# One Trainium2 kernel re-planned: engine order from an in-kernel list scheduler, DMA transposes, and attention outputs computed in column tiles

## Chip, cores, metric

One core of one Trainium2 chip. The metric is device time in microseconds (us) of one launch. Medians are quoted with the range of the runs. The record calls a run slow when it lies over 1.5% above the fastest run of its kernel in the same call.

Engine names in the profile: PE is TensorE's matmul stream, PEld its weight loads, DVE is VectorE, ACT is ScalarE, POOL is GpSimd, SP is SyncE.

## The reference, cut to what matters

Two branches read the same x (2048 tokens of 512) and are mixed by a gate per token. All inputs are bf16.

```python
def reference(A_x, A_wq, A_wk, A_wv, A_wo, A_beta, B_x, B_W_gate, B_W_up, B_W_down, gate_w):
    # branch A: 32 heads of 16, four segments of 512 tokens
    for s in range(4):
        logits = einsum('bhqd,bhkd->bhqk', qs, ks) * scale + mask    # causal, within the segment
        a_dot  = einsum('bhqk,bhkd->bhqd', softmax(logits), vs)
        pq     = phi(qs)                                 # phi(t) = t+1 if t>0 else exp(t)
        a_mem  = (pq @ M) / (pq @ z + 1e-6)              # recall from the state so far
        o      = g * a_mem + (1.0 - g) * a_dot           # g = sigmoid(beta), per head
        M, z   = M + phi(ks)^T @ vs, z + sum(phi(ks))    # the state
    a = concat(o) @ wo
    # branch B: a gated feed-forward of width 1792
    b = (relu(x @ W_gate) * (x @ W_up)) @ W_down
    g = sigmoid((x * gate_w).sum(-1, keepdims=True))     # per token
    return g * a + (1 - g) * b
```

Three groups of work follow from this. Dense matmuls are the projections, the feed-forward and the output projection. Attention is the scores ("QK"), their exponential, and the product with V ("PV"). The rest is the state, its recall, and the norm. A "unit" is one segment and one group of eight heads; there are 16.

## The kernel before: the parts that the change touches

PV uses the exponentials as weights and streams V (17 columns, one of them ones, which gives the softmax denominator). The norm and a matmul that transposes its result follow for each of 64 blocks.

```python
        for qb in range(4):
            ndt = psum.tile([P, NDT], F32, name="ndt", tag="X", bufs=2)
            # ... recall matmul into ndt, for segments after the first
            for hl8 in range(8):
                for kb in range(qb + 1):
                    nc.tensor.matmul(ndm[:, 0, hl8, 0:DH + 1],
                                     lhsT=E[kb][:, es, (qb - kb) * P:(qb - kb + 1) * P],
                                     rhs=st["Vp"][:, kb, h, 0:DH + 1], start=first, stop=last)
            # ... VectorE: + eps, reciprocal, * gate, * numerator, sum  ->  o_sb
            nc.tensor.matmul(trp, lhsT=o_sb.rearrange("p h e -> p (h e)"),
                             rhs=diag16[:, t, :], start=True, stop=True)
            nc.vector.tensor_copy(oT[:, c, qb * P:(qb + 1) * P], trp)
```

phi(K) for the state needs tokens on partitions, so K is projected a second time, with x as the weight:

```python
            for t in range(4):
                for ci in range(NC):
                    nc.tensor.matmul(ps[:], lhsT=xT[:, ci, s0 + t * P:s0 + (t + 1) * P],
                                     rhs=wk_sb[:, ci, :], start=(ci == 0), stop=(ci == NC - 1))
                # ... exponential, min, max-add  ->  pK
```

x is transposed by 64 matmuls, and the loads are spread over three queues:

```python
    load_x(nc.sync, 0)
    load_w_piece(nc.scalar, wq_sb, A_wq, 0, D)
    load_w_piece(nc.scalar, wk_sb, A_wk, 0, D)
    load_w_piece(nc.scalar, wv_sb, A_wv, 0, D)
    load_w_piece(nc.sync, wg_sb, B_W_gate, *FP[0])
    load_w_piece(nc.sync, wu_sb, B_W_up, *FP[0])
    load_x(nc.gpsimd, 1)
    # ... the other pieces alternate between the SP and the GpSimd queue
```

The order of each engine's instructions is chosen by the framework, from the order in which the program writes them.

The softmax here doesn't subtract the row's maximum and nothing guards it: scores larger than these inputs give would overflow.

## Time and profile before

| | before |
|---|---|
| time, median (range) | 354.35 us (354.02 to 354.99) |
| span of the profiled run, mean granted clock | 351.7 us, 0.993 |
| busy: PE / DVE / ACT / POOL | 308.4 / 229.1 / 198.0 / 90.5 us |
| first dense matmul at full supply | after a 5.0 us wait that ends at 19.03 us |

How to read it: the span is from the first instruction to the last of the core; the reported time is a little longer (1.7 to 2.0 us in the runs for which both are on record). TensorE is the fullest engine. Its busy time counts a dense matmul of 512 columns as 0.38 us in this trace, while the next one starts after 0.216 us, so a full TensorE must be read from the distance between starts. The lines are in the prediction below.

### The profile page before, as it was taken

How to read it: one execution, taken by the hardware profiler on the slowest of the kernel's cores; microseconds unless marked ns; L12 is line 12 of the kernel's file. 1: busy time of each engine (PE TensorE's matmuls, PEld its weight loads, DVE VectorE, ACT ScalarE, POOL GpSimd, SP SyncE). 2: the span in 40 equal slices, each digit the busy share in tenths (PEclk: the TensorE clock that was granted, in tenths of full speed). 3: DMA queues.
4: the chain of work that ended last, by engine and by line, in shares of the span. 5: the costliest groups of instructions: out<-in, count | busy, mean ns of one | idle time of the engine just before them, and what ended most of it. 6: DMA issues, size and time to landing. Idle time of an engine off the chain costs nothing.

```text
span 351.7 us, 7235 instructions
## 1 busy us (share of the span) xinstructions
PE 308.4 (88%) x2941; PEld 148.1 (42%) x2992; DVE 229.1 (65%) x684; ACT 198.0 (56%) x187; POOL 90.5 (26%) x153
## 2 busy tenths in 40 slices
PE   3489988899999799898999988888999989989984
PEld 2133343335444344334644444334544444444452
DVE  2557959788422756989835575899845386766253
ACT  1306578755843687831754577841764378886300
POOL 6000343341321424310231144230231133242300
PEclk9989999999999999999999999999999999999999
DMA  7991100001000000001000000000000000000000
GB/s 195 357 335 55 61 2 0 2 1 62 3 16 16 32 2 0 2 0 61 2 2 17 30 18 3 0 2 0 2 3 17 30 17 2 0 2 3 0 32 30
DMA packets 10209, 12.39 MB, mean 35 GB/s; under 512 B 593, under 2 KB 9313, under 8 KB 10177
## 3 DMA queue, kind: packets, MB, share of 16 engines
q1 hardware_dynamic: 7584, 6.82, 6.1%
q0 software_dynamic: 1008, 3.55, 3.3%
q10 hardware_dynamic: 1584, 1.57, 1.4%
q8 instruction: 23, 0.38, 0.4%
q14 instruction: 10, 0.07, 0.1%
HBM read 9.84 MB, written 2.10 MB: 34 GB/s over the span
## 4 chain that ended last, share of the span: by engine, by line
PE 52%; DVE 30%; ACT 7%; DMA 5%; issue 3%; POOL 0%; SPq 0%; DVEq 0%; ACTq 0%
PE acc L398 14%; PE ups L383 9%; PE gps L378 7%; PE ndt L317 6%; DMA wu_sb<-in_B_W_up_dram 5%; PE sp L255 4%; DVE hT L388 4%; DVE tb L339 3%; DVE osb L411 3%; PE ps_proj L242 2%; PE ndt L343 2%; PE acc L408 2%; DVE coef L337 2%; PE ps_proj L230 2%; DVE rsb L335 2%
## 5 line engine op out<-in xcount | busy, mean ns | idle before, releaser
L383 PE MATMUL ups<-xT,wu_sb 128*128 128x512 bf16 x210 | 62.7, 382 | 7.1 <-DMA wu_sb<-in_B_W_up_dram 5.0
L378 PE MATMUL gps<-xT,wg_sb 128*128 128x512 bf16 x205 | 59.8, 380 | 2.3 <-DMA wg_sb<-in_B_W_gate_dram 1.0
L388 DVE TENSOR_TENSOR hT<-ups,rg 128x512 bf16<-128x512 f32 x56 | 38.3, 684 | 24.2 <-PE ups L383 18.5
L387 ACT ACTIVATE rg<-gps 128x512 bf16<-128x512 f32 x56 | 33.5, 598 | 35.7 <-PE gps L378 27.8
L398 PE MATMUL acc<-wd_sb,hT 128*128 128x512 bf16 x217 | 50.3, 379 | 0.9 <-DVE osb L411 0.2
L398 PEld LDWEIGHTS <-hT 128*128 128x128 bf16 x224 | 21.5, 98 | 25.3 <-issue 1.2
L383 PEld LDWEIGHTS <-wu_sb 128*128 128x128 bf16 x224 | 20.1, 98 | 25.5 <-DMA wu_sb<-in_B_W_up_dram 5.5
L345 DVE CAST oT<-ndt 128x128 bf16<-128x128 f32 x64 | 18.3, 286 | 16.4 <-PE ndt L343 16.4
L411 DVE TENSOR_SCALAR osb<-acc,ngcol 128x512 bf16<-128x512 f32 x16 | 12.0, 750 | 22.5 <-PE acc L408 22.5
L378 PEld LDWEIGHTS <-wg_sb 128*128 128x128 bf16 x224 | 18.3, 97 | 18.2 <-issue 3.7
L343 PE MATMUL ndt<-diag_134,o_sb 128*128 128x128 bf16 x64 | 14.5, 226 | 11.4 <-DVE o_sb L342 9.8
L333 DVE TENSOR_TENSOR dsb<-ndt,epsvec 128x16 f32<-128x16 f32 x48 | 8.1, 169 | 24.2 <-PE ndt L317 23.7
L255 PE MATMUL sp<-QTsb,KTe 32*128 32x512 bf16 (+3 forms) x256 | 21.7, 304 | 0.7 <-issue 0.2
L339 DVE TENSOR_TENSOR tb<-ndt,coef 128x256 bf16<-128x256 f32 x48 | 20.2, 421 | 1.3
L255 PE MATMUL sp<-QTsb,KTo 32*128 32x512 bf16 (+3 forms) x256 | 20.2, 299 | 0.6 <-ACT E_3100 L276 0.2
L408 PE MATMUL acc<-wo_sb,oT 128*128 128x512 bf16 x60 | 17.8, 380 | 2.3 <-DVE oT L345 1.9
L218 PE MATMUL ps_proj<-xT,wk_sb 128*128 128x512 bf16 x64 | 17.1, 396 | 2.3 <-DVE KTe L221 0.9
L242 PE MATMUL ps_proj<-wv_sb,xT 128*128 128x512 bf16 x62 | 15.7, 379 | 2.6 <-DVE pK L236 1.1
L343 PEld LDWEIGHTS <-o_sb 128*128 128x128 bf16 x64 | 6.1, 95 | 27.6 <-DVE o_sb L342 23.1
L204 PE MATMUL ps_proj<-xT,wq_sb 128*128 128x512 bf16 x61 | 17.1, 393 | 0.5
L255 PEld LDWEIGHTS <-KTe 32*128 32x128 bf16 x256 | 7.1, 91 | 24.1 <-issue 22.9
L207 DVE CAST QTsb<-ps_proj 128x512 bf16<-128x512 f32 x16 | 10.8, 685 | 3.8 <-PE ps_proj L204 3.8
(468 smaller groups left out, 708.6 us busy)
## 6 DMA issues: line engine op xcount, KB each, us to landing
out_dram<-osb SPq DMA_DIRECT2D x16, 128.0 KB, 1.7
xn<-in_A_x_dram POOLq DMA_DIRECT2D x3, 512.0 KB, 3.8
wd_sb<-in_B_W_down_dram POOLq DMA_DIRECT2D x2, 640.0 KB, 12.4
wg_sb<-in_B_W_gate_dram SPq DMA_DIRECT2D x2, 512.0 KB, 14.2
wu_sb<-in_B_W_up_dram SPq DMA_DIRECT2D x2, 512.0 KB, 18.2
wg_sb<-in_B_W_gate_dram SPq DMA_DIRECT2D x2, 384.0 KB, 13.2
wu_sb<-in_B_W_up_dram SPq DMA_DIRECT2D x2, 384.0 KB, 8.8
xn<-in_A_x_dram SPq DMA_DIRECT2D x1, 512.0 KB, 4.9
```

What stands on the lines that cost most here:

```text
L242: nc.tensor.matmul(ps[:], lhsT=xT[:, ci, s0 + t * P:s0 + (t + 1) * P], rhs=wv_sb[:, ci, :], start=(ci == 0), stop=(ci == NC - 1))
L255: nc.tensor.matmul(out_ap, lhsT=ktile[32 * j:32 * j + 32, c, kb * P:(kb + 1) * P], rhs=st["QTsb"][32 * j:32 * j + 32, c, kb * P:kb * P + N ...
L317: nc.tensor.matmul(ndm[:, 0, hl8, 0:DH + 1], lhsT=E[kb][:, es, (qb - kb) * P:(qb - kb + 1) * P], rhs=st["Vp"][:, kb, h, 0:DH + 1], start=f ...
L339: nc.vector.tensor_tensor(tb[:], ndm[:, :, :, 0:DH], coef[:, :, :, None].to_broadcast([P, 2, 8, DH]), ALU.mult)
L343: nc.tensor.matmul(trp, lhsT=o_sb.rearrange("p h e -> p (h e)"), rhs=diag16[:, t, :], start=True, stop=True)
L378: nc.tensor.matmul(gps[:], lhsT=wg_sb[:, ci, fv * P:(fv + 1) * P], rhs=xT[:, ci, s0:s0 + L], start=(ci == 0), stop=(ci == NC - 1))
L383: nc.tensor.matmul(ups[:], lhsT=wu_sb[:, ci, fv * P:(fv + 1) * P], rhs=xT[:, ci, s0:s0 + L], start=(ci == 0), stop=(ci == NC - 1))
L387: nc.scalar.activation(rg[:], gps[:], ACT.Relu)
L388: nc.vector.tensor_tensor(hT[:, fv, :], ups[:], rg[:], ALU.mult)
L398: nc.tensor.matmul(acc[:], lhsT=hT[:, fv, lc:lc + P], rhs=wd_sb[:, fv, :], start=(fv == 0), stop=False)
L408: nc.tensor.matmul(acc[:], lhsT=oT[:, ci, lc:lc + P], rhs=wo_sb[:, ci, :], start=False, stop=(ci == NC - 1))
L411: nc.vector.tensor_scalar(osb[:], acc[:], ngcol[:, tt:tt + 1], None, ALU.mult)
```

## The change

Its intent: take work off TensorE's stream (second K projection, most transposes of x, the transposes of the normalised output), get PV done four heads at a time, move the norm off TensorE's path, and replace the framework's ordering by a plan. The kernel describes each piece of work as an operation with assumed durations, dependences and buffers. A list scheduler inside the kernel plans all engines, and the instructions are then emitted in that order with the framework's own ordering switched off ("pinned").

The diff replaces nearly the whole file. Its core, with cuts marked:

```diff
+class Sched:                       # list scheduler: engines, dependences, buffers, mode changes
+    LAT = {"PE": 0.30, "ACT": 0.12, "DVE": 0.12, "POOL": 0.15, "SP": 0.0, "ACTQ": 0.0}
+    # ... run(): earliest start first; TensorE by key, a change of tile mode costs SW = 0.1
...
+    def c_dummy(e):                # TensorE: ten matmuls on zeros while the loads come
+        for _ in range(10):
+            nc.tensor.matmul(g_dummy.t[:], lhsT=zero[:, 0:P], rhs=zero[:], start=True, stop=True)
...
+    lw["wq"] = loadw("wq", wq_sb, A_wq, 0, D, -200, eng="ACT")      # order: x0, wq, wk, wv, then
+    lw["wk"] = loadw("wk", wk_sb, A_wk, 0, D, 1)                    # gate/up pieces, x1, wo, wd
...
+            nc.sync.dma_start_transpose(out=xT[s].t[:], in_=x[s * L:(s + 1) * L, :])   # s = 1..3
...
-                    nc.tensor.matmul(ps[:], lhsT=xT[:, ci, s0 + t * P:s0 + (t + 1) * P],
-                                     rhs=wk_sb[:, ci, :],             # second K projection
+                nc.sync.dma_start_transpose(out=pK[s].t[:, :, c * P:(c + 1) * P], in_=src.t[:])
...
-                    nc.tensor.matmul(ndm[:, 0, hl8, 0:DH + 1],
-                        lhsT=E[kb][:, es, (qb - kb) * P:(qb - kb + 1) * P],
-                        rhs=st["Vp"][:, kb, h, 0:DH + 1], start=first, stop=last)
+                for kb, src, off, w in ((0, ea, 0, 512), (1, ebf, 0, 384),
+                                        (2, ec, 256 * r, 256), (3, ebf, 384, 128)):
+                    for j in range(4):
+                        h = 8 * c + 2 * j + r
+                        nc.tensor.matmul(g.t[32 * j:32 * j + 32, L - w:L],
+                                         lhsT=Vp[s].t[:, kb, h * HP:h * HP + 32],
+                                         rhs=src.t[:, j, off:off + w],
+                                         start=(kb == 0), stop=(kb == 3), tile_position=(0, 32 * j))
...
-            nc.tensor.matmul(trp, lhsT=o_sb.rearrange("p h e -> p (h e)"),
-                             rhs=diag16[:, t, :], start=True, stop=True)
+                    nc.vector.transpose(T.t[:, r, :, :].rearrange("p b e -> p (b e)"), g.t[:])
+            # ... reciprocal, * gate, * numerator on VectorE, then
+            nc.vector.transpose(dst.t[:], Oa.t[:].rearrange("p b r e -> p (b r e)"))
...
+    order = sc.run()
+    with tc.manual_schedule():
+        for o in order:
+            o.emit(o.eng)
```

In the changed kernel's profile, L439 are projections and gate/up matmuls, L574 the down projection, L584 the output projection, L625 the scores, L656 PV, L670 the recall, L518 the state, L343 the transposes of x by TensorE, L261 the matmuls on zeros; L635 is the exponential, L561 the product of gate and up, L689 VectorE's transpose from PSUM.

## The prediction

> **What bounds the kernel now.** I read the page's busy line first, then the busy slices, then the table of stretches, the matmul timeline and the list of waits.
>
> ```profile
> PE 308.4 (88%) x2941; PEld 148.1 (42%) x2992; DVE 229.1 (65%) x684; ACT 198.0 (56%) x187; POOL 90.5 (26%) x153
> PE   3489988899999799898999988888999989989984
> PEclk9989999999999999999999999999999999999999
> ```
>
> TensorE is busy in nearly every slice, and its granted clock is full. But a modelled matmul time (380 ns for 512 columns) overlaps the next one, so 308 us is not work. The timeline gives the true pace:
>
> ```profile
> 120.77 0.23 PE L343 MATMUL ndt<-diag_134,o_sb 128*128 128x128 bf16 x1 [1.40 <-DVE o_sb L342]
> 120.84 1.03 PE L378 MATMUL gps<-xT,wg_sb 128*128 128x512 bf16 x4
> 121.70 0.81 PE L383 MATMUL ups<-xT,wu_sb 128*128 128x512 bf16 x3
> ...
> 128.68 0.81 PE L378 MATMUL gps<-xT,wg_sb 128*128 128x512 bf16 x2
> 129.42 0.29 PE L255 MATMUL sp<-QTsb,KTe 32*128 32x256 bf16 x4
> 129.54 0.28 PE L255 MATMUL sp<-QTsb,KTo 32*128 32x256 bf16 x4
> 129.75 0.39 PE L378 MATMUL gps<-xT,wg_sb 128*128 128x512 bf16 x1
> ```
>
> Start to start, four dense 512-column matmuls take 121.70 - 120.84 = 0.86 us, 0.215 each. Four QK matmuls of 32 rows and 256 columns take 129.54 - 129.42 = 0.12 us: they run side by side, at the price of one. The second four take 0.21 us to the next dense matmul, 0.10 more: that is the change of tile mode. On entry, the last dense matmul before starts at 128.68 + 0.81 - 0.38 = 129.11 and streams to 129.33, so 0.09 is lost there too. I use 0.1 us per change, either way.
>
> PV is 1280 matmuls of 17 columns. Sixteen of them lie between these two starts:
>
> ```profile
> 123.06 0.17 PE L317 MATMUL ndt<-Vp,E_1344 128*128 128x17 bf16 x1
> ...
> 123.47 1.02 PE L378 MATMUL gps<-xT,wg_sb 128*128 128x512 bf16 x4
> ```
>
> 0.41 us / 16 = 0.025 us each. With these prices, and counts from the code and the instruction order: dense 976 x 0.216 = 210.8; QK 16 units x 1280 columns x 2 = 17.3; its 202 mode changes 20.2; PV 1280 x 0.025 = 32; the 64 transposes of x, 64 of o_sb, 48 recall and 48 state matmuls, at about 0.06, together 14. Sum 294 us of a 351.7 us span. The other 57 us are waits, in two places:
>
> ```profile
> 0.00:19.00 19.00, 7.22 (x36) 3.66 (x36) 7.25 (x26) 4.41 (x7) 6.12 (x20) 1.00 0.92 281
> 104.00:189.00 85.00, 77.83 (x761) 38.04 (x774) 57.95 (x176) 50.81 (x49) 21.17 (x34) 1.00 0.04 14
> ```
> ```profile
> PE ndt L343 <- DVE o_sb L342: 9.8, 17, 1.4
> PE tp L174 <- DMA xn<-in_A_x_dram: 5.7, 1, 5.7
> PE ups L383 <- DMA wu_sb<-in_B_W_up_dram: 5.0, 1, 5.0
> ```
>
> (In the stretches the columns are length, busy PE, PEld, DVE, ACT, POOL, clock, DMA share, GB/s.) The first 19 us hold 20 dense matmuls and 16 transposes, some 5.3 us: 13.7 us are lost to loads, while DMA is 92% busy. TensorE follows a fixed order that asks for an up-projection weight before it has landed. Later the normalisation sits inside TensorE's order: PV, then five VectorE instructions, then a matmul that transposes their result, 64 times; TensorE stands at that matmul. The remaining 40 us are these and many small waits of a fixed order.
>
> [...]
>
> **The change, part by part.** The computation is the same; these are TensorE's costs in the changed kernel.
>
> *State from transposed phi(k).* The second K projection (48 dense matmuls) goes; 12 DMA transposes of 128x512 take its place. Dense is then 928 x 0.216 = 200.4: 10.4 us less, all in TensorE's time. x of segments 1 to 3 is transposed by DMA too: 48 of 64 transposes and 12 of 16 evictions go, 3 us of TensorE. DMA moves 14 GB/s in mid-kernel, so there is room.
>
> *QK.* The scores are packed into five full fills of 4 x 512 columns per unit in place of six of mixed size: 80 x 0.216 = 17.3, unchanged, as the same columns stream.
>
> *PV in column tiles.* V (32 columns with its ones) is the weight, the scores stream, four heads at once. Per unit 2 x 1280 columns; if the four run side by side as row tiles do, 2 x 0.55 us, x16 = 17.6 in place of 32. It adds mode changes: the order of the changed kernel has 213, 21.3 us against 20.2.
>
> *Recall.* 24 x 512 columns, 5.2 us in place of 3. *State* 2.9, unchanged. *The 64 o_sb transposes by matmul* go (4 us of streaming and, more, the waits): VectorE makes 32x32 transposes before and after the norm, whose result is first read by the output projection, much later.
>
> Sum: 200.4 + 17.3 + 17.6 + 21.3 + 5.2 + 2.9 + 1.0 (transposes of segment 0) = 266 us, 28 us less than the 294.
>
> *Head.* x, wq and wk (1.5 MB) now come ahead of the rest; at the 357 GB/s of the page's second slice that is 4.2 us, plus about 2 us to first landing. Ten matmuls on zeros fill the wait and, if it works, warm the clock. I put 8 us in place of 13.7. *Tail:* output scaling 0.75 us and a store at 1.7 us to landing, with their handovers 4 us, as before.
>
> *ScalarE.* From rows of the trace: 80 exponentials of 2048 elements at 1.877 = 150; 56 relu at 0.598 = 33.5; 24 phi exponentials 14.4; 23 evictions taken over from VectorE at 0.6 = 14; 12 output scalings 8.4. About 222 us, up from 198. *VectorE:* 56 gate products at 0.684 = 38; 56 fp32 transposes from PSUM, put at the same 0.68 = 38; 28 norm products of 512 elements 19; 16 bf16 transposes 10; phi about 16; 25 evictions 17; token gate 12; the rest some 45. About 195, down from 229. Both stay below TensorE.
>
> *The pinned order.* A list scheduler with durations close to the trace's (1.88, 0.69, 0.62, 0.75, a mode change of 0.1) fixes each engine's order. It cannot make work shorter. It should take most of the 40 us of small waits, but in-order engines wait wherever a true time is longer than the assumed one, and ScalarE leaves little slack: with one score buffer each exponential waits for its fill and each fill for the exponential before. I leave 10 us, a quarter of today's waits. That is the least certain term.
>
> Span: 266 + 8 + 4 + 10 = 288. The reported time is 2.6 us above the span now (354.35 - 351.7); the terms for head and stalls are rounded up, so I take 287.
>
> **Rivals.** (a) *Column tiles do not run side by side, or their weights are not hidden.* [...] Against it: the row tiles hide theirs, although they too are loaded tile by tile (mean 91 ns each). If wholly serial, 32 x 4 x 0.55 = 70 us in place of 17.6, and about 340 us: nearly no gain. If only the loads show, at a quarter of today's 98 ns each, 512 x 0.025 = 13 us, and 300. (b) *ScalarE becomes the bound.* 222 us of work; in the trace a gap of about 0.6 us stands before an exponential that waits for its fill. If half of 80 gaps stay unfilled, 24 us: 246 + start 11 + end 12 = 269, still under 287, but waits of two nearly full engines add up; 295 to 300. (c) *DMA transposes are slow.* [...]phi(k) has two buffers, so VectorE could stand in its order behind a transpose[...]. (d) *The scheduler's plan holds nearly exactly:* stalls of 2 to 3 us, 279.
>
> **Range and chances.** Main line 287; (d) sets the lower end, with a better head 275; (b) and the mild form of (a) the upper end, 304. Only serial column tiles come near the old time, and the 2% line is 347. Faster by over 2%: 0.97; within 2%: 0.02; slower: 0.01.
>
> **What would show it.** Right: PV of one half unit takes 0.5 to 0.6 us start to start, mode changes 0.1; no wait of TensorE on a VectorE norm; first dense matmul near 7 us at full pace; ScalarE busy about 222 us and VectorE about 195; TensorE's waits summing to 20 to 25 us. Wrong: PV blocks of 2 us (a); fills that start late because of ScalarE (b); VectorE or loads behind DMA transposes (c); or TensorE losing far more than 10 us between head and tail for reasons not in this list.

## The result, and the profile after

| | before | after |
|---|---|---|
| time, median (range) | 354.19 us (353.50 to 354.99) | 294.03 us (291.03 to 295.27) |
| ratio | 1 | 0.829, 95% interval 0.8243 to 0.8337 |
| span of the profiled run | 351.7 us | 289.0 us |
| busy: PE / DVE / ACT / POOL | 308.4 / 229.1 / 198.0 / 90.5 us | 274.0 / 203.3 / 213.4 / 93.6 us |

Ratios here and below are the mean time of one kernel's fast runs over that of the other's of the same rounds, so not quite the ratio of the medians that are quoted.

The page after: busy time of each engine, TensorE's busy tenths in 40 slices, and the chain that ended last by engine.

```profile
PE 274.0 (95%) x2050; PEld 111.0 (38%) x2050; DVE 203.3 (70%) x484; ACT 213.4 (74%) x204; POOL 93.6 (32%) x141
PE   8999788999969999999999999999999999996995
PE 82%; DVE 11%; ACT 3%; issue 3%; POOL 0%; POOLq 0%; ACTq 0%; DVEq 0%
```

TensorE is now the chain itself, to 82%. The low slices are the head, dips between 29 and 51 us, near 83 and near 264 us, and the end.

The table of stretches after (columns: length, busy PE, PEld, DVE, ACT, POOL, clock, DMA share, GB/s):

```profile
88.00:168.00 80.00, 79.72 (x617) 31.75 (x615) 63.87 (x145) 63.19 (x57) 27.55 (x41) 1.00 0.08 18
168.00:248.00 80.00, 80.00 (x608) 31.67 (x607) 50.44 (x101) 61.95 (x55) 26.10 (x40) 1.00 0.03 11
```

For 160 us TensorE hardly stops. Before, 85 us of the middle held 77.8 us of its busy time.

The matmul timeline after, at one PV block, and at the head (start, duration, what, in brackets the wait and its releaser):

```profile
1.25 4.45 PE L261 MATMUL G<-os 128*128 128x512 bf16 x10 [1.25 <-DVE os L225]
7.71 1.02 PE L439 MATMUL G<-xT,wq_sb 128*128 128x512 bf16 x4 [0.61 <-DVE xT L350]
8.57 0.59 PE L439 MATMUL G<-xT,wk_sb 128*128 128x512 bf16 x2
...
22.49 0.73 PE L656 MATMUL G<-E,Vp 128*32 128x512 bf16 x16
23.15 0.40 PE L625 MATMUL S<-QT,KO 32*128 32x384 bf16 x8
```

The 16 matmuls of a PV block, 4 x 1280 columns, take 23.15 - 22.49 = 0.66 us with their mode change: 0.56 without it. Four heads side by side would stream 1280 columns at 0.216 us per 512, which is 0.54. The first dense group starts at 7.71 and takes 8.57 - 7.71 = 0.86 us, the full pace at once.

The list of TensorE's waits after (total, times, longest):

```profile
PE G L439 <- DVE hT L561: 3.5, 2, 1.8
PE S L625 <- ACT E L635: 2.7, 2, 2.0
PE G L518 <- DVE hT L561: 2.0, 1, 2.0
PE G L261 <- DVE os L225: 1.3, 1, 1.3
```

What is not shown of the list is under 1 us each, of which 0.2 us is on the first step of the norm (L689). The waits of 1.4 us on the norm are gone, and none on a weight is left. What is left are a few waits of about 2 us on VectorE and ScalarE.

A count from start to start over the whole timeline divides the span of 289.0 us: 7.7 before the first dense matmul, 245.9 of streaming, 20.7 of mode changes (213, at 0.10), 11.2 of waits, 3.6 from the end of the last stream to the end of the span. The matching prediction was 8 + 1.0, 243.4, 21.3, 10 and 4.

The table of DMA issues after (count, KB each, us from issue to landing; transposes show no size):

```profile
xn<-in_A_x_dram SPq DMA_DIRECT2D x3, 512.0 KB, 5.0
pK<-pk SPq DMA_TRANSPOSE x12, 2.4
xT<-in_A_x_dram SPq DMA_TRANSPOSE x3, 5.1
```

A transposing load of a segment takes 5.1 us where the ordinary load of the same 512 KB takes 5.0, so transposing on the way cost these loads 0.1 us.

Where the 62.7 us of span came from: TensorE's stream with its mode changes fell from an estimated 294 us (the prediction's sum) to 266.6, and everything else fell from 57.7 to 22.4. The stream gives 27 us, the waits, head and tail 35. The experiments split the 35, though only in part.

### The profile page after: what moved, and what is told of

It is laid out like the page before. It is cut to its first block, busy times and chain, and to the rows that moved or that the text cites. A ratio compares the mean times of both kernels' runs of the same rounds, so it can differ in the third digit from the quotient of the medians.

```text
span 289.0 us, 5294 instructions
## 1 busy us (share of the span) xinstructions
PE 274.0 (95%) x2050; PEld 111.0 (38%) x2050; DVE 203.3 (70%) x484; ACT 213.4 (74%) x204; POOL 93.6 (32%) x141
## 4 chain that ended last, share of the span: by engine, by line
PE 82%; DVE 11%; ACT 3%; issue 3%; POOL 0%; POOLq 0%; ACTq 0%; DVEq 0%
PE G L439 43%; PE G L574 15%; PE S L625 8%; PE G L656 6%; PE G L584 5%; DVE R L414 3%; ACT E L635 3%; DVE hT L561 3%; DVE xn L397 2%; PE G L261 2%; PE G L670 1%; DVE T L689 1%; PE G L343 0%; POOL E L642 0%; DVE O L703 0%
## 5 line engine op out<-in xcount | busy, mean ns | idle before, releaser
L635 ACT ACTIVATE E<-S 128x2048 bf16<-128x2048 f32 x80 | 150.0, 1875 | 38.8 <-PE S L625 36.1
L642 POOL TENSOR_SCALAR_AFFINE_SELECT E<-E 128x512 bf16<-128x512 bf16 x128 | 86.2, 688 | 181.3 <-ACT E L635 176.1
L439 PE MATMUL G<-xT,wu_sb 128*128 128x512 bf16 x224 | 57.8, 380 | 1.8 <-DVE hT L561 1.7
L439 PE MATMUL G<-xT,wg_sb 128*128 128x512 bf16 x224 | 57.7, 380 | 1.8 <-DVE hT L561 1.8
L561 DVE TENSOR_TENSOR hT<-G,rg 128x512 bf16<-128x512 f32 x56 | 38.0, 681 | 29.8 <-PE G L439 19.0
L689 DVE STREAM_TRANSPOSE T<-G 128x512 f32<-128x512 f32 x56 | 39.2, 705 | 23.4 <-PE G L656 22.9
L574 PE MATMUL G<-wd_sb,hT 128*128 128x512 bf16 x224 | 53.6, 380 | 0.0
L557 ACT ACTIVATE rg<-G 128x512 bf16<-128x512 f32 x56 | 33.2, 597 | 8.0 <-PE G L439 7.7
L439 PEld LDWEIGHTS <-wg_sb 128*128 128x128 bf16 x224 | 20.4, 98 | 27.5 <-issue 5.8
L439 PEld LDWEIGHTS <-wu_sb 128*128 128x128 bf16 x224 | 19.5, 98 | 27.3 <-issue 7.8
L574 PEld LDWEIGHTS <-hT 128*128 128x128 bf16 x224 | 20.1, 98 | 25.4 <-issue 4.3
L656 PE MATMUL G<-E,Vp 128*32 128x256 bf16 (+3 forms) x512 | 23.6, 302 | 0.5 <-DVE T L689 0.2
L703 DVE TENSOR_TENSOR O<-T,sm 128x512 bf16<-128x512 f32 x28 | 21.7, 776 | 0.4
L625 PE MATMUL S<-QT,KO 32*128 32x256 bf16 (+3 forms) x256 | 17.1, 300 | 2.0 <-ACT E L635 2.0
L656 PEld LDWEIGHTS <-Vp 128*32 128x32 bf16 x512 | 10.8, 96 | 19.1 <-issue 11.0
L625 PE MATMUL S<-QT,KT 16*128 16x512 bf16 (+3 forms) x256 | 17.3, 302 | 0.9 <-ACT E L635 0.7
L439 PE MATMUL G<-xT,wq_sb 128*128 128x512 bf16 x64 | 16.5, 380 | 0.6 <-DVE xT L350 0.6
L439 PE MATMUL G<-xT,wk_sb 128*128 128x512 bf16 x64 | 16.5, 380 | 0.0
L584 PE MATMUL G<-wo_sb,oT 128*128 128x512 bf16 x64 | 16.2, 380 | 0.0
L439 PE MATMUL G<-wv_sb,xT 128*128 128x512 bf16 x64 | 15.7, 380 | 0.0
```

Source lines behind the costliest of these rows:

```text
L439: nc.tensor.matmul(g.t[:], lhsT=lhs(ci), rhs=rhs(ci), start=(ci == 0), stop=(ci == NC - 1))
L557: nc.scalar.activation(rg.t[:], g.t[:], ACT.Relu)
L561: nc.vector.tensor_tensor(h.t[:], u.t[:], rg.t[:], ALU.mult)
L574: nc.tensor.matmul(g.t[:], lhsT=hT[s, fb].t[:, t * P:(t + 1) * P], rhs=wd_sb[:, fb, :], start=(fb == 0), stop=False)
L584: nc.tensor.matmul(g.t[:], lhsT=oT[s, c].t[:, t * P:(t + 1) * P], rhs=wo_sb[:, c, :], start=False, stop=(c == NC - 1))
L625: nc.tensor.matmul(sp.t[:, j, off:off + w], lhsT=ks[rows, kb * P:(kb + 1) * P], rhs=QT[s, c].t[rows, q0:L], start=True, stop=True, tile_po ...
```

## The experiments

Twelve kernels ran, in three calls. As the changed kernel's time varies from run to run, I compare with its seven fast runs (four of the result, three of the first experiment): mean 292.8 us, range 290.34 to 295.27. The three calls ran on different chips, and of them the changed kernel was in the first alone. The kernel before, which ran in each, had a mean of 354.0 us in the first and 353.6 us in the other two, so differences across calls are good to about 0.5 us.

### 1. The changed kernel again

No edit. 

> The changed kernel once more, so that the others of this call have it on the same chip. Expected ratio to before 0.83 (first run 0.829), about 294 us.

Measured: 292.61 us median (290.34 to 295.88), ratio 0.8243. With the four of the result, eight runs fall into two groups. Three have a granted clock of 1.000 and take 290.34 to 291.03 us; five have 0.982 to 0.988 and take 293.36 to 295.88 (the last is the slow one). The first profile was of the first group, so it shows no low clock. The profile of this experiment, of a run of 294.51 us, shows where the clock falls. Its table of stretches, columns as before:

```profile
83.00:85.00 2.00, 1.89 (x16) 0.88 (x15) 1.97 (x10) 1.04 (x1) 0.00 (x0) 0.95 0.00 0
85.00:88.00 3.00, 2.74 (x27) 1.02 (x28) 2.83 (x6) 1.68 (x2) 0.63 (x1) 0.50 0.00 0
...
43.80:47.20 3.40, 3.18 (x10) 1.27 (x10) 3.40 (x10) 0.69 (x2) 1.36 (x2) 0.51 0.00 0
269.10:272.50 3.40, 3.18 (x24) 1.19 (x22) 1.78 (x2) 1.88 (x1) 2.19 (x3) 0.50 0.01 2
```

At 83.1 us TensorE ends a wait of 2.0 us on VectorE (L561). 1.7 us later the clock falls to 0.50 for about 3.4 us, although TensorE is busy by then. The same happens at 43.8 and at 269.1 us, each time less than 0.2 us after a wait of 1.8 or 2.0 us ends. The first profile has waits of the same lengths and no such fall. So these waits may have cost more than their length: the three falls stand beside a span of 292.5 us in place of 289.0, some 1.2 us each. Over the fast runs the groups differ by 294.5 - 290.7 = 3.8 us. Only this one of the five runs with a lower clock has a profile.

### 2. PV with the heads in the outer loop

```diff
-                for kb, src, off, w in ((0, ea, 0, 512), ...):
-                    for j in range(4):
+                for j in range(4):
+                    for kb, src, off, w in ((0, ea, 0, 512), ...):
```

> PV with the head as outer and the key block as inner loop: same 512 matmuls, same results, but four in a row now sit in the same column tile. Theory (column tiles run side by side only when neighbours in order lie in different tiles): a block of 16 goes from 0.66 us start to start, its mode change in it, to 4 x 0.55 + 0.1 = 2.3 us, so 32 x 1.6 = 52 us more TensorE work and about 345 us: nearly the time of before. Rival ([...]the gain of PV came from fewer matmuls alone): a block stays below 1 us and the time within 5 us of the changed kernel.

Measured: 293.82 us (293.14 to 295.29), ratio 0.8304. The matmul timeline of this run:

```profile
58.11 0.76 PE L656 MATMUL G<-E,Vp 128*32 128x512 bf16 x16
58.80 1.04 PE L439 MATMUL G<-wv_sb,xT 128*128 128x512 bf16 x3
```

The block takes 0.69 us, not 2.3. My theory that neighbours in the order must be on different column tiles falls. The four tiles run side by side in both orders that were tried. It was a failed attempt to make PV serial; the size of PV is tested in experiment 5.

### 3. The same emission order, not pinned

```diff
-    with tc.manual_schedule():
-        for o in order:
-            o.emit(o.eng)
+    for o in order:
+        o.emit(o.eng)
```

> The same operations emitted in the same list order, but without the pin: the framework's own scheduler orders each engine, as it did in the kernel before. Theory 1 (most of the small waits went because the norm left TensorE's order, not because of the pin): at most 10 us slower than the changed kernel, about 300 us. Theory 2 (the pinned order is what removed the 30 us of waits): 20 to 35 us slower, 315 to 330 us, with waits of TensorE in the list that sum to over 30 us.

Measured: 311.83 us (310.10 to 313.43), ratio 0.8791: mean 311.8, so 19.0 us over the changed kernel and between the theories. Comparing the two traces by line, operation and tile, 2034 of TensorE's 2050 weight loads stand in the same order, but only 325 of VectorE's 484 instructions. The head shows what that does; timeline of VectorE, then of TensorE, then a line of the table of stretches:

```profile
10.80 0.18 DVE L377 TENSOR_SCALAR gbt<-eb 128x32 f32<-128x32 f32 x1 [7.49 <-ACT eb L373]
```
```profile
14.86 1.87 PE L439 MATMUL G<-xT,wq_sb 128*128 128x512 bf16 x4 [8.35 <-DVE xT L350]
16.51 1.56 PE L439 MATMUL G<-xT,wk_sb 128*128 128x512 bf16 x4
```
```profile
10.80:17.50 6.70, 2.65 (x7) 1.03 (x8) 5.14 (x23) 1.64 (x4) 0.00 (x0) 0.50 1.21 281
```

VectorE stands for 7.5 us at an operation of the head gates, whose input waits for a small load that lands at about 10.5 us. Copies of x stand behind it, so the first dense matmul starts at 14.86 in place of 7.71, and at half pace (1.65 us to the next group); the granted clock is 0.50 in this stretch. The remaining 12 us go with more waits of TensorE on VectorE and ScalarE and a lower clock (0.972 to 0.983), which I did not separate. Pinning is worth about 19 us here, and the order of VectorE is what it protects above all. What pinning would do to the kernel before is untested.

### 4. The measured durations in the scheduler

The plan assumed durations for VectorE that the trace does not bear out. Only the assumed numbers change, and with them the order:

```diff
-        b = op(f"R{s}", {"DVE": 1.1}, f, deps=[a], key=kz + 4)
+        b = op(f"R{s}", {"DVE": 3.4}, f, deps=[a], key=kz + 4)
-            zo.append(op(f"z{s}{t}", {"DVE": 0.62}, ...
+            zo.append(op(f"z{s}{t}", {"DVE": 0.89}, ...
-            a = op(f"pr{s}{c}.{kind}", {"DVE": 0.62}, ...
+            a = op(f"pr{s}{c}.{kind}", {"DVE": 0.80}, ...
# ... head gates 1.4 -> 2.3, clamp 0.08 -> 0.28, phi 0.65 -> 0.88, norm 0.5 -> 0.6 or 0.85, and six smaller ones
```

> Only the durations that the list scheduler assumes for VectorE are changed, to those measured in the changed kernel's profile (the sixteen copies of the token gate 3.4 us in place of 1.1, norm product 0.80 for 0.62, and so on). The instructions are the same, only their order moves. Theory (the waits near 34, 44, 48 and 82 us come of VectorE durations that were assumed too short, so that TensorE arrives at an operation whose input is late): these four, 7 us in all, shrink to below 3 and the time falls by 2 to 5 us. Rival (VectorE is simply full in these stretches, and no order helps): within 2 us of the changed kernel, with the waits elsewhere.

The reason for this test is in the changed kernel's timeline of VectorE, before TensorE's wait that ends at 33.77 us (last line):

```profile
29.95 1.41 DVE L414 COPY R<-rcol 32x4 f32<-32x4 f32 x8
...
31.99 1.12 DVE L397 CUSTOM_DVE_ANT_0 xn<-xn,gwrep 128x512 bf16<-128x512 bf16 x1
...
33.04 0.68 DVE L561 TENSOR_TENSOR hT<-G,rg 128x512 bf16<-128x512 f32 x1
33.77 1.02 PE L439 MATMUL G<-xT,wu_sb 128*128 128x512 bf16 x4 [1.69 <-DVE hT L561]
```

The little copies cost 0.18 us each here (0.20 in the mean of 64), where the plan had 1.1 us for 16, which is 0.07. VectorE was behind its plan, and the product that frees TensorE's PSUM buffer stood behind the token gate; TensorE waited 1.7 us for it.

Measured: 285.38 us (283.70 to 287.04), ratio 0.806: 7.5 us less in the means, more than the 2 to 5 us of the theory. Of runs with clock 1.000 it is 283.70 against 290.34 to 291.03, so about 7 us are not a matter of the clock. In the profiles TensorE's listed waits after the head fall from 9.2 to 5.0 us and its mode changes from 213 to 201; the rest of the 7 us I have not itemised. TensorE's waits in this run:

```profile
PE S L625 <- ACT E L635: 3.1, 4, 2.0
...
PE G L439 <- DVE hT L561: 0.3, 1, 0.3
```

The waits on L561 fell from 5.5 us to 0.3. Most of what is left is at the end.

### 5. PV twice

Each PV block is issued twice. The second pass starts its sums anew (`start` is set again at `kb == 0`), so the result stays right.

```diff
-                for kb, src, off, w in ((0, ea, 0, 512), ...):
+                for kb, src, off, w in 2 * ((0, ea, 0, 512), ...):
```

> Each PV block of 16 matmuls runs twice, the second pass overwriting the first (same result). The order assumed by the scheduler is unchanged. Theory (TensorE's stream is the bound, and a PV block costs 5120 columns over four tiles, 0.55 us): 32 x 0.55 = 17.6 us more, 310 us, minus what goes into waits that are there anyway, so 14 to 18 us over the changed kernel; a block lasts 1.2 us start to start. Rival (TensorE has slack; ScalarE's chain of fills and exponentials sets the pace): under 8 us more.

Measured: 309.60 us (308.99 to 310.17), ratio 0.8753, 16.7 us over the changed kernel's mean. In this run's timeline the block of 32 takes 61.47 - 60.27 = 1.20 us; 0.54 more than 0.66, times 32 blocks, is 17.3. Nearly all of the added streaming is added time: TensorE's stream is the bound, and a second PV costs about what was predicted for the first (17.6).

```profile
60.27 1.27 PE L656 MATMUL G<-E,Vp 128*32 128x512 bf16 x32
61.47 0.82 PE L439 MATMUL G<-wv_sb,xT 128*128 128x512 bf16 x2
```

### 6. The second K projection back

```diff
-                nc.sync.dma_start_transpose(out=pK[s].t[:, :, c * P:(c + 1) * P], in_=src.t[:])
+        a = op(f"p{s}{t}", {"PE": 4 * MM},
+               mm4(g, lambda ci: xT[s].t[:, ci, t * P:(t + 1) * P], lambda ci: wk_sb[:, ci, :]), ...
# ... and its exponential, min and max-add, as in the kernel before
```

> The second K projection is back: 48 dense matmuls, exponential from PSUM, two VectorE instructions, in place of 12 DMA transposes of phi(k); scheduled again by the same scheduler. The prediction put this part at 10.4 us of TensorE time. Theory (TensorE bound): 6 to 11 us slower than the changed kernel, about 301 us; less than the full 10.4 only where the extra matmuls fill waits, of which the end of the kernel has 3 to 4 us. Rival (the DMA transposes cost as much in waits of VectorE and the DMA queue as they save): within 3 us, or faster.

Measured: 298.19 us (297.51 to 303.06), ratio 0.8431. The mean of the three fast runs is 298.0, 5.1 us over, just under the theory's 6 to 11; the run of 303.06 is slow. The stream grows by 48 dense matmuls, an estimated 10.4 us from 0.216 each, and the time by half of that. But the three fast runs have a clock of 0.999 to 1.000; against the changed kernel's runs of that clock (290.7) the difference is 7.3 us. In this profile TensorE's 2.7 us of waits on the last exponentials are gone; more feed-forward matmuls lie between the last scores there, which is probably why. So the part is worth its 10.4 us of stream, but 5 to 7 us of time in this plan.

### 7. One matmul on zeros in place of ten

```diff
-        for _ in range(10):
+        for _ in range(1):
```

> One matmul on zeros at the start in place of ten. Theory (the ten warm the clock while the first loads are under way; without them the first 3 to 4 us of real matmuls run at half the pace, as the first ones of the kernel before do, 0.43 us each): the first dense matmul starts at the same time, within 0.5 us, the first group of four takes 1.7 us in place of 0.86, and the time is 1.5 to 2.5 us longer. Rival (the zeros matter for nothing, or the clock opens by itself): within 0.5 us.

Measured: 293.49 us (292.07 to 294.72), ratio 0.8297; in the medians no difference. The timeline shows one:

```profile
7.25 1.87 PE L439 MATMUL G<-xT,wq_sb 128*128 128x512 bf16 x4 [0.61 <-DVE xT L350]
8.91 1.58 PE L439 MATMUL G<-xT,wk_sb 128*128 128x512 bf16 x4
10.33 1.03 PE L439 MATMUL G<-xT,wq_sb 128*128 128x512 bf16 x4
```

The first two groups of four take 1.66 and 1.42 us in place of 0.86 each, 1.36 us lost; as the first starts 0.46 earlier than with ten, the third group is 0.9 us behind. With ten, the half pace falls on the zeros themselves, ten in 4.24 us (1.25 to 5.49 us of the changed kernel's profile, 0.42 us each). Runs of clock 1.000 are 292.07 and 292.32 against 290.34 to 291.03, 1.5 us in the means. So the ten matmuls on zeros are worth 1 to 1.5 us; the spread of the clock hides it in the medians.

### 8. A plan tuned by hand

The durations of experiment 4, the 64 little copies on GpSimd, units 13.75 us apart in the order keys in place of 15, and scores preferred right after PV.

```diff
+                        if o.mode == "R" and mode == "C":
+                            k -= 6.0
-    TA0, PU = 9.0, 15.0
+    TA0, PU = 9.0, 13.75
-                    nc.vector.tensor_copy(R[s][32 * j:32 * j + 32, :, k], rcol[32 * k:32 * k + 32, cols])
+                    nc.gpsimd.tensor_copy(R[s][32 * j:32 * j + 32, :, k], rcol[32 * k:32 * k + 32, cols])
```

> A version meant to beat both: measured VectorE durations in the scheduler as in a4, the 64 small copies of the token gate moved from VectorE to GpSimd, the attention units planned 13.75 us apart in place of 15 so that the last exponentials come before dense work runs out, and a QK fill preferred directly behind a PV block. Theory (what is left are waits on VectorE and a stall of some 4 us at the end where three fills in a row wait for ScalarE): 277 to 283 us, with no wait of TensorE over 1 us at the end. Rival (the small GpSimd copies delay the masks, and PV with them; or ScalarE is the bound already): no faster than a4, 285 us.

Measured: 278.95 us (278.64 to 279.76), ratio 0.7891. It beats both kernels. The granted clock is 1.000 in all four runs, and TensorE's only waits are 2.1 us, of which 1.9 are in the head.

### 9. Durations and keys only

Experiment 8 changed four things. This kernel has the measured durations and two order keys, nothing else:

```diff
-    TA0, PU = 9.0, 15.0
+    TA0, PU = 9.0, 14.25
-    STR = 1.25
+    STR = 1.2
```

> The changed kernel with the measured VectorE durations in its scheduler (the run before that did only this took 285.4 us), and with the order keys of the last PV groups moved a little earlier (14.25 in place of 15, and 1.2 in place of 1.25), which should let the last tile's scores come before the last exponentials are waited for. My theory: what is left of that run over a full stream are waits of TensorE on ScalarE's exponential at the end, together 3 us, and the lower clock after them; then this kernel takes 279 to 282 us, with under 1 us of waits at the end and no low slice of the clock there. Rival: the end is bound by ScalarE's own work, and moving the groups moves the wait; then it stays within 2 us of 285.4.

Measured: 278.59 us (278.33 to 278.67), ratio 0.7877, the fastest kernel here, level with experiment 8. Its list of TensorE's waits:

```profile
...
PE S L625 <- ACT E L635: 0.2, 1, 0.2
```

Above it stand only the 1.3 and 0.6 us of the head. The wait on the last exponentials went from 3.1 to 0.2 us, and the profile has no low clock (the runs have 0.998 to 1.000). The rival, that ScalarE's own work binds the end, falls. One caution: the keys reorder TensorE throughout, not only at the end, so the 6.8 us against experiment 4 are the worth of this plan, of which the seen end waits are 2.9 us.

### 10. The little copies on GpSimd only

The measured durations, and the one line of experiment 8 that moves the copies.

> The changed kernel with the measured VectorE durations in its scheduler, and with the 64 little copies of the norm (together 12.8 us of VectorE) on GpSimd. Theory: with true durations the plan already goes round VectorE's load, so taking 12.8 us off it gains at most 3 us over the 285.4 us of the run with true durations alone: 282 to 286 us. Rival: VectorE's bursts still hold TensorE up; then it falls by 4 to 6 us, to about 280.

Measured: 284.36 us (282.88 to 284.46), ratio 0.8032: 1.0 us under experiment 4 in the median, for 12.8 us less of VectorE; experiment 4's own runs are 3.3 us apart. With true durations the plan goes round VectorE's load. As experiment 9 is level with experiment 8 without moving the copies, the gain of experiment 8 is that of keys and durations.

### 11. The kernel before with another order of loads

```diff
-    load_w_piece(nc.scalar, wk_sb, A_wk, 0, D)
-    load_w_piece(nc.scalar, wv_sb, A_wv, 0, D)
-    # ... pieces of wg, wu on SP between x1..x3, wo, wd on GpSimd
+    load_w_piece(nc.sync, wk_sb, A_wk, 0, D)
+    load_w_piece(nc.sync, wv_sb, A_wv, 0, D)
+    for i in range(4):
+        load_w_piece(nc.sync, wg_sb, B_W_gate, *FP[i])
+        load_w_piece(nc.sync, wu_sb, B_W_up, *FP[i])
+    load_w_piece(nc.sync, wo_sb, A_wo, 0, D)
+    # ... wd on SP, x1..x3 on GpSimd
```

> The kernel before, untouched but for the order of its loads: segment 0 of x and the K and V weights first on the SP queue, the Q weights on the ACT queue, then the gate and up pieces, and the later segments of x on GpSimd's queue. In the kernel before, TensorE started its first dense matmul after about 14 us. Theory: about 5 of the 60 us come from the order of the loads alone; then this kernel takes 346 to 349 us. Rival: the head is hidden by the work that the framework puts there, or the later stages then wait for the up weights as they did; then it is within 2 us of the kernel before, 352 to 355 us.

Measured: 347.82 us (347.57 to 349.76), ratio 0.9849: 5.3 us less in the means. That is clear of the noise (95% interval 0.9815 to 0.9882). One figure of my expectation was wrong: the kernel before starts its first dense matmul at 7.24 us, not 14; what the loads cost it there is the waits that follow. The wait of 5.0 us on the up weights is gone; the largest after the first load is now this one, in TensorE's timeline:

```profile
12.76 0.82 PE L367 MATMUL gps<-xT,wg_sb 128*128 128x512 bf16 x3 [1.43 <-DMA wg_sb<-in_B_W_gate_dram]
```

The mean clock of the profiled run rose from 0.993 to 0.999. The order of the loads is worth about 5 us by itself, without any other part of the change.

### 12. x of all segments transposed by TensorE

```diff
-            nc.sync.dma_start_transpose(out=xT[s].t[:], in_=x[s * L:(s + 1) * L, :])
+                for c in range(NC):
+                    nc.tensor.transpose(gv[:, c * P:(c + 1) * P], xn[s].t[:, t, c * P:(c + 1) * P], ident[:])
# ... and the copies out of PSUM, for s = 1..3 as for s = 0
```

> The changed kernel with x of all four segments transposed by TensorE, as it is for segment 0, in place of the DMA transposes of segments 1 to 3: 48 more transposes of 128 columns, 12 more copies out of PSUM, mostly on VectorE. Theory: TensorE's stream is the bound, so its added work is added to the time: 48 of about 0.06 us and up to 12 mode changes of 0.10 us each, with some copies waited for: 296 to 300 us. Rival: this work falls into waits that exist already, and the time stays at 291 to 295 us.

Measured: 298.55 us (298.06 to 300.08), ratio 0.8451, 6.0 us over the changed kernel's mean, and 4.5 over its two fast runs of the same clock (0.988). This run failed the check of its result, with a relative error of 0.0200; I did not look for the cause, and use the run only for the time of its instruction stream. The transposes add an estimated 3 us to TensorE (48 at 0.06), and waits that the changed kernel does not have, from the list of waits:

```profile
PE G L343 <- DVE hT L557: 2.8, 1, 2.8
...
PE G L343 <- DMA xn<-in_A_x_dram: 1.5, 1, 1.5
```

So the DMA transposes of x seem worth somewhat more than their matmuls, as the copies out of PSUM and the plain loads bring waits of their own. With a wrong result behind it, this stays a hint.

### What the runs add up to

| kernel | median us | mean clock of the runs | mean of fast runs against the changed kernel's |
|---|---|---|---|
| before | 353.4 to 354.2 | 0.989 to 0.994 | +61 |
| before, other load order | 347.82 | 0.995 to 0.999 | |
| not pinned | 311.83 | 0.972 to 0.983 | +19.0 |
| PV twice | 309.60 | 0.988 to 0.994 | +16.7 |
| second K projection back | 298.19 | 0.987 to 1.000 | +5.1 |
| x by TensorE (wrong result) | 298.55 | 0.988 to 0.989 | +6.0 |
| heads outermost in PV | 293.82 | 0.988 to 0.994 | +1.2 |
| one matmul on zeros | 293.49 | 0.988 to 1.000 | +0.6 |
| the change | 294.03, 292.61 | 0.982 to 1.000 | 0 |
| measured durations | 285.38 | 0.988 to 1.000 | -7.5 |
| and copies on GpSimd | 284.36 | 0.994 to 1.000 | -8.8 |
| tuned by hand | 278.95 | 1.000 | -13.8 |
| measured durations, two keys | 278.59 | 0.998 to 1.000 | -14.3 |

Of the 61 us, then: about 27 are less streaming (by the prediction's estimate of the stream before and the count of the stream after); about 19 are pinning; the other 15 are shared by the norm that left TensorE's order, the order of the loads (5 us when done alone on the kernel before) and the warm start (1 to 1.5 us). These parts are not independent, as experiments 3 and 6 show, so the whole split is an attribution, not a measurement. Neither the norm's part nor the column tiles were undone by themselves; for the norm there are only the 9.8 us of waits in the prediction's list.

## Why the prediction was right, and where it missed

The range (275 to 304) held; 294.03 stands against 287.

*The stream* was right. Predicted 243.4 us of streaming without the head's transposes and 21.3 of mode changes; counted 245.9 and 20.7. The price of a dense matmul of 512 columns held: four take 0.86 us, and the long dense stretches here stay at 0.216 us each.

*Rival (a), column tiles that run serially or show their loads,* is refuted. A block took 0.56 us against 0.55 predicted, with 16 weight loads of 96 ns in it. One after another its 5120 columns would take an estimated 2.16 us, at 0.216 per 512, and its loads alone 1.5; so the four tiles worked in parallel, and the loads cost nothing that can be seen in these 0.56 us. The dense loads of 98 ns did not show at 0.216 us per matmul either. Experiment 5 shows that the time follows PV's stream.

*Rival (b), ScalarE as the bound,* is refuted. ScalarE was busy for 213.4 us; the rows of its groups sum to 224, near the predicted 222, as busy time counts overlapping ends once. Even in the kernel of 278.6 us it waits 29 us for its fills, and TensorE 0.2 us for it. In the changed kernel TensorE waited 2.7 us for exponentials at the end, which a better order removed (experiment 9).

*Rival (c), slow DMA transposes,* is refuted by 2.4 and 5.1 us to landing, and by the absence of TensorE waits on them.

*Rival (d), a plan that holds nearly exactly,* gave 279 and was kept as the lower end. The changed kernel did not reach it; its plan with true VectorE durations and two other keys did, at 278.6. There the span of 276.9 is 7.1 of head, about 246 of stream, 20.0 of 200 mode changes and 3.6 of tail: nothing is left to wait for.

*The term called least certain,* 10 us of stalls, measured 11.2. It came from the cause that the prediction named: "in-order engines wait wherever a true time is longer than the assumed one". The cause was right (TensorE's 1.7 us at 33.77 us, in experiment 4, is such a wait); the size was a guess (a quarter of today's 40), so its nearness is partly luck. Yet the prediction called the durations "close to the trace's", which failed for VectorE, above all for operations that the kernel before did not have: the 64 little copies at 0.20 us in place of 0.07. VectorE's transposes of 128x512, new as well, took 705 ns from fp32 in PSUM and 694 ns for bf16. VectorE's rows then sum to about 221 us, and its busy time to 203, against 195. Which instructions a mis-stated duration would hold up could have been asked before: the scheduler's numbers were in the diff, and small VectorE operations had durations in the trace before (0.17 to 0.25 us for those of 128x16).

*The miss of 7 us* has three parts. The span was 1.0 above the predicted 288. The step from span to time was wrong by 3.0: the prediction subtracted one for rounding where the trace has 2.0 to add (291.03 against 289.0). Its 2.6 us for the kernel before set a median against the span of another run; where both are on record they differ by 1.7 to 2.0. The last 3.0, the median against the run of full clock, has no term in the prediction at all. It said "its granted clock is full" of the kernel before and carried this over. But five of eight runs had a lower clock, and in the one with a profile it fell to 0.50 after waits of about 2 us. The kernel before has one such fall as well, for 3.4 us from 19.4 on, after its wait of 5.0 us.

*Single parts:* the state from transposed phi(K) was put at 10.4 us "all in TensorE's time". That is right for the stream, but undoing it costs 5 to 7 us (experiment 6). The head (8 + 1.0 us, measured 7.7) and the tail (4 us, measured 3.6) held.

## What to carry to other kernels

A plan that pins the order of all engines is as good as its durations: replace every assumed one by the trace's, then rerun the plan, before tuning anything else. When TensorE is the bound, price each part by start-to-start distances, and take its worth in time from undoing it, since a removed matmul may only open a wait (10.4 us of stream were worth 5 to 7 us of time in experiment 6). Compare runs of the same granted clock: in one run the clock fell to 0.50 after each of three waits of about 2 us, beside a span 3.5 us longer, and this spread hides effects of 1 to 2 us in the medians.
